# Unit 0's squares on VectorE, 1/(2 pi) inside the triangular factor, late caps and roundings on ScalarE, and a new written order of steps

## The chip, the cores and the metric

The kernel runs on one core of a Trainium2 chip. Times are microseconds (us) of that core for one execution; lower is better. Engines are named as the profile names them: PE is TensorE (PEld its weight loads), ACT is ScalarE, DVE is VectorE, POOL is GpSimd and SP is SyncE, which here only issues DMAs. A "q" behind a name (SPq, POOLq) is that engine's own instruction queue.

## The reference

```python
# gates: q, k, v, a_re, a_im are (4, 8, 768, 48) float32
mag = np.sqrt(a_re * a_re + a_im * a_im)
scale = np.minimum(mag, 0.999) / (mag + 1e-06)
a_re_n, a_im_n = (a_re * scale, a_im * scale)
for t in range(S):                         # S = 768 steps
    new_re = ar * S_re - ai * S_im
    new_im = ar * S_im + ai * S_re
    kv = np.einsum('bhd,bhe->bhde', k[:, :, t], v[:, :, t])
    S_re, S_im = (new_re + kv, new_im)
    y[:, :, t] = np.einsum('bhd,bhde->bhe', q[:, :, t], S_re)
...
x = y.transpose(0, 2, 1, 3).reshape(3072, 384)
h = x @ w_in                               # (384, 2048), float64 in memory
sp = log(1 + exp(h))
out = (h * erf(sp)) @ w_out                # (2048, 384)
```

The first part is a linear recurrence with complex gates per head and channel; the second is a feed-forward layer whose activation is h times the error function of softplus(h).

## The kernel before

**Units.** The 3072 tokens are cut into 12 units u = 0 to 11 of 256 tokens, each of two chunks c of 128 tokens (one token per partition, 8 heads x 48 channels = 384 elements along the free axis). Three units make one sequence of 768 tokens. The recurrence becomes prefix sums: the logarithms of the gate magnitudes and the gate angles are summed over the tokens of a chunk by a matmul with an upper triangular matrix of ones, `triu`, and then exponentials and sines of those sums weight q and k, so that a chunk's result is two small matmuls per head.

**The steps of one unit.** Every step is a Python generator that issues one or a few instructions each time it is resumed.

- `g` loads the real and imaginary gate parts (`ar`, `ai`) for a chunk, `k`, `q`, `v` the inputs.
- `m` (`g_mag`) squares both on ACT and adds them on DVE: s = |a|^2, with a sum for the final check.
- `t` (`g_tan`), `o`, `r` (`g_turn`): ai/ar by a logarithm, an exponential and a product, its largest value, and the arctangent, which leaves the angle in `th`.
- `l` (`g_log`): ln of s, then on DVE the cap `min(0.5 ln s, ln 0.999)` (L951, a tensor_scalar) and a subtraction (L953). From unit 5 on (`HALVED`) it also splits s into a rounded part `hi` (L958) and a rest `lo` (L960), so that the prefix sum can run as two matmuls in the float32r type with `triu_r`, a rounded copy of `triu`.
- `a` (`g_angle`): divides `th` by 2 pi (ACT, L991, units 0 to 4; from unit 5 on L984 together with the split), takes the prefix sum and removes whole turns. `p` (`g_decay`): prefix sum of s and two exponentials. `s` (`g_sin`): cosine and sine.
- `K`, `Q`, then `kT`/`qT` (transposes on PE, units 0 and 1) or `M` (transposes through DMAs, later units), `A` (scores), `S` (state), `Y` (result, gives xT).
- `h` (`ff_in`): x @ w_in, two tiles of 128 x 256 per resumption on PE and a copy to SBUF on ACT. Eight such tiles are a slab `sl`; two slabs make the 2048 hidden channels.
- `x` (`softplus`): four ACT passes over a whole slab, 128 x 2048: exp, ln, ln, exp. `e` (`erf_times_h`): one Gelu on ACT and four products on DVE per 128 x 512.
- `O`: the second matmul. Units 0 to 2 do it directly; units 3 to 11 by Strassen-like sums (`f`, banks X, Y, Z, W), and the last of these steps write the output.
- `n`, `b`, `i`: turn the float64 weights into float32, form sums of weights, and look once more through the weights for a check. `u` (`warm`): matmuls of the identity with itself whose result nobody reads, 48 of them, all near the start. `Z` (`check`): sums all check values and writes one flag `ok`; at the end every engine loads `ok` and branches past a slower general path.

**The order.** Nothing is scheduled by a tool. `ORDER` is a string of some 2290 step names, and the kernel resumes the named step each time:

```python
for nm in ORDER.split():
    if nm[0] == "u":
        steps[nm] = warm(int(nm[1:].split("_")[0]))
    next(steps[nm])
```

Each engine then runs its own instructions strictly in that order, with semaphores where data or buffers are awaited. DMAs are issued by SP, apart from the two first `ai` loads, which ACT issues (L801). Buffers of the gate stage (`lda`, `tmp`, `gat`) exist once, so a load into `ar` or `ai` waits until the previous unit's last reader is done. The first h matmuls need four converted pieces of w_in. ACT functions come in three table sets, and `act` loads a set (L785) when the next function is in another one.

Of the kernel before, what the change touches and what calls it, by code (L numbers as in the profile page):

```python
# [10 lines left out]
FP = mybir.dt.float32  # L11
# [38 lines left out]
u8_0 u2_40 u2_41 g0.0 g0.0 u4_38 u4_21 g0.1 g0.1 u4_20 u2_39 u4_2 t0.0 t0.0 t0.0 m0.0 m0.0 m0.0 m0.1 l0.0 t0.1  # L50
m0.1 m0.1 l0.0 l0.0 l0.0 l0.1 t0.1 l0.1 l0.1 l0.0 u2_25 p0.0 p0.0 p0.0 u2_34 u2_22 u8_1 o0.0 r0.0 a0.0 t0.1 l0.1
o0.1 r0.1 a0.1 n0 n0 n0 l0.1 n0 a0.0 a0.0 p0.1 n1 n1 n1 a0.0 a0.1 u2_24 g1.0 u2_23 k0.0 g1.0 q0.0 K0.0 m1.0 m1.0
n1 m1.0 s0.0 s0.0 s0.0 Q0.0 Q0.0 qT0.0.0 K0.0 v0.0 p0.0 v0.1 q0.1 k0.1 qT0.0.1 kT0.0.1 t1.0 p0.1 a0.1 p0.1 a0.1
t1.0 qT0.0.0 kT0.0.1 kT0.0.0 t1.0 o1.0 r1.0 qT0.0.1 kT0.0.0 g1.1 g1.1 Q0.1 S0.0 p0.0 K0.1 A0.0.0 A0.0.0 S0.0
s0.1 A0.0.1 A0.0.1 a1.0 a1.0 n3 p0.1 n2 p0.1 s0.1 s0.1 K0.1 Q0.1 n3 kT0.1.0 m1.1 m1.1 m1.1 n3 t1.1 l1.0 kT0.1.0
a1.0 l1.0 l1.1 a1.0 S0.1 S0.1 l1.0 l1.1 S0.1 qT0.1.1 qT0.1.1 t1.1 kT0.1.1 kT0.1.1 Y0.0 qT0.1.0 l1.1 qT0.1.0 l1.0
l1.0 p1.0 p1.0 Y0.0 p1.0 t1.1 n3 o1.1 r1.1 s1.0 a1.1 s1.0 A0.1.1 A0.1.1 A0.1.0 A0.1.0 Y0.1 q1.0 k1.0 K1.0 l1.1
q1.1 g2.0 v1.1 n4 l1.1 n2 n2 n2 s1.0 Q1.0 Q1.0 g2.1 v1.0 g2.1 g2.0 k1.1 a1.1 n6 n5 p1.0 n7 Y0.1 p1.1 K1.0 t2
a1.1 m2 n4 a1.1 n4 h0.0.6 t2 m2 m2 h0.0.4 p1.1 h0.0.6 n4 Q1.1 n6 t2 o2 p1.1 K1.1 l2 s1.1 l2 h0.0.4 l2 l2 r2 l2
n6 n6 kT1.0.0 kT1.0.0 h0.0.2 h0.1.0 h0.0.2 s1.1 s1.1 p1.1 q2.0 k2.0 a2.0 qT1.0.0 kT1.0.1 p2.0 qT1.0.0 n7 n7 a2.0  # L60
p2.0 p2.0 a2.0 n7 h0.0.0 h0.1.0 h0.0.0 kT1.0.1 qT1.0.1 qT1.0.1 a2.0 a2.0 x0.0 x0.0 e0.0.2 e0.0.0 n5 n5 g3.0 g3.0
n9 n8 n5 a2.0 a2.1 p1.0 p1.1 k2.1 v2.1 q2.1 S1.0 K1.1 A1.0.0 A1.0.1 Q1.1 A1.0.1 A1.0.0 a2.1 a2.1 h0.1.6 h0.1.6
Y1.0 v3.0 qT1.1.1 qT1.1.1 qT1.1.0 qT1.1.0 Y1.0 n8 n8 S1.0 n8 S1.0 n9 n9 a2.1 a2.1 a2.1 kT1.1.0 kT1.1.0 n9
kT1.1.1 kT1.1.1 S1.1 S1.1 S1.1 K2.0 Q2.0 p2.1 A1.1.1 A1.1.1 A1.1.0 A1.1.0 h0.1.4 s2 s2 s2 K2.0 Q2.0 g3.1 g3.1
Q2.0 n10 K2.0 n10 p2.0 v2.0 t3 m3 m3 m3 t3 h0.1.4 t3 o3 p2.1 p2.1 K2.1 n10 n10 Y1.1 l3 Y1.1 n11 h0.1.2 r3 h0.1.2
S2.0 p2.0 h1.0.0 M2.0 g4.1 M2.0 M2.0 k3.0 M2.0 g4.0 g4.0 S2.0 n11 K2.1 a3.0 a3.0 l3 S2.0 Q2.1 h1.0.0 l3 a3.0 l3
Q2.1 a3.0 l3 a3.1 n11 Q2.1 K2.1 h1.1.0 h1.0.2 x0.0 h1.1.0 x0.0 p3.1 p3.1 a3.1 p3.1 a3.1 p3.0 p3.0 A2.0.1 A2.0.0
e0.0.2 e0.0.0 e0.0.2 e0.0.2 e0.0.0 e0.0.0 A2.0.0 A2.0.1 n11 e0.0.2 m4 e0.0.0 h1.0.2 a3.1 a3.1 a3.1 t4 g4.1 m4
p3.0 t4 t4 h1.0.4 e0.0.6 e0.0.6 h1.0.4 h1.0.6 h1.0.6 Y2.0 q3.0 n12 g5.1 h1.1.2 n15 g5.0 M2.1 M2.1 M2.1 M2.1
e0.0.4 e0.0.4 e0.0.6 n12 e0.0.4 e0.0.4 e0.0.6 e0.0.4 h1.1.6 s3 s3 O0.1 s3 O0.0 e0.0.6 O0.2 O0.3 A2.1.1 A2.1.0  # L70
O0.4 O0.5 O0.6 x0.1 Q3.0 m4 l4 x0.1 l4 x0.1 l4 x0.1 K3.0 Q3.0 n12 n12 K3.0 n15 l4 K3.0 o4 l4 p3.0 k3.1 a4.0 p3.1
p3.0 A2.1.1 K3.1 A2.1.0 Y2.1 Q3.0 e0.1.2 e0.1.2 e0.1.0 e0.1.0 e0.1.2 Y2.0 h1.1.2 r4 e0.1.0 e0.1.2 e0.1.0 e0.1.2
a4.0 e0.1.0 e0.1.6 h1.1.6 Y2.1 e0.1.6 e0.1.6 e0.1.4 e0.1.4 e0.1.4 n15 a4.0 O0.7 S3.0 h1.1.4 h1.1.4 n15 x1.0 x1.0
# [12 lines left out]
Q4.1 O0.14 q5.0 p4.1 g6.0 K4.1 a5.1 a5.1 a5.1 a5.1 a5.1 e2.0.4 S4.1 A4.0.1 A4.0.0 A4.0.0 x2.1 e2.1.2 e2.1.2
e2.1.2 e2.1.2 g6.1 a5.1 h3.0.2 e2.1.2 m6 e2.1.0 e2.1.0 e2.1.0 e2.1.0 e2.1.0 O1.15 a5.1 g6.0 g6.1 k5.0 k5.1 O1.14
Y4.0 O1.14 h3.0.4 h3.0.6 O2.1 h3.0.0 O2.3 O2.5 O2.7 M4.1 M4.1 M4.1 M4.1 A4.1.1 A4.1.0 Y4.0 m6 h3.0.6 e2.1.4
e2.1.6 s5 s5 m6 e2.1.4 e2.1.6 e2.1.4 e2.1.4 e2.1.6 S4.1 s5 Q5.0 Q5.0 K5.0 K5.0 A4.1.1 K5.1 e2.1.6 e2.1.6 l6
h3.0.0 l6 t6 t6 q5.1 A4.1.0 x3.0 x3.0 l6 t6 S5.0 h3.1.4 h3.1.4 Q5.0 Q5.1 K5.0 l6 l6 K5.1 S5.0 l6 l6 e2.1.4 x3.0  # L90
x3.0 o6 Y4.1 e3.0.2 e3.0.2 e3.0.2 e3.0.0 e3.0.0 e3.0.2 e3.0.0 e3.0.2 e3.0.0 e3.0.0 h3.1.0 h3.1.0 r6 a6.0 Y4.1
a6.0 e3.0.6 e3.0.6 e3.0.6 e3.0.4 e3.0.4 e3.0.4 O1.14 v5.1 p5.0 M5.0 M5.0 M5.0 M5.0 q6.0 O2.9 h3.1.6 O2.0 O2.2
h3.1.2 h3.1.6 h3.1.2 a6.0 a6.0 a6.0 Q5.1 K5.1 e3.0.6 a6.1 a6.1 p5.0 e3.0.4 e3.0.4 A5.0.0 A5.0.0 O2.4 O2.6 A5.0.1
O2.8 O2.10 x3.1 x3.1 a6.1 x3.1 O2.12 A5.0.1 Y5.0 Q5.1 O1.15 M5.1 M5.1 x3.1 Y5.0 a6.1 a6.1 b6 e3.0.6 f3.0 b0 S5.0
b2 a6.1 a6.1 f3.0 e3.1.2 e3.1.0 h4.0.0 p6.0 e3.1.2 e3.1.0 e3.1.2 e3.1.2 h4.0.0 e3.1.0 e3.1.0 e3.1.2 e3.1.0 p6.0
Q6.0 p6.1 O2.14 O2.14 p6.0 e3.1.6 e3.1.6 e3.1.4 e3.1.4 e3.1.6 e3.1.4 e3.1.6 e3.1.6 e3.1.4 e3.1.4 s6 p6.1 p6.1
g7.0 k6.0 g7.1 m7 g7.1 g7.0 v7.0 i0 p6.0 i1 M5.1 M5.1 p6.1 h4.0.2 h4.0.2 m7 O2.11 O2.13 O2.15 t7 O2.15 t7 h4.0.6
h4.0.6 b0 b4 b6 m7 b6 b0 l7 l7 b0 b4 i0 b4 f3.1 b4 p6.0 h4.0.4 h4.0.4 l7 x4.0 x4.0 l7 i1 l7 b2 l7 l7 a7.0 h4.1.6
h4.1.6 O3.1 O3.1 t7 o7 h4.1.0 A5.1.1 O3.2 A5.1.0 A5.1.0 A5.1.1 b2 O3.2 f3.1 O3.0 O3.3 O3.4 h4.1.4 Y5.1 x4.0 x4.0
p6.1 v6.0 O2.14 q6.1 O2.15 e4.0.0 e4.0.0 e4.0.0 b2 e4.0.2 e4.0.2 e4.0.0 e4.0.2 e4.0.0 e4.0.2 r7 a7.0 e4.0.2 s6  # L100
s6 h4.1.0 e4.0.6 e4.0.6 e4.0.6 e4.0.4 e4.0.4 a7.0 a7.0 e4.0.4 h4.1.2 Y5.1 h4.1.4 h4.1.2 x4.1 O3.5 a7.0 a7.0 x4.1
k6.1 b6 O3.6 O3.7 e4.0.6 e4.0.4 h5.0.4 O3.5 O3.5 e4.0.4 O3.5 O3.7 a7.0 O3.7 a7.1 O3.4 x4.1 x4.1 K6.0 e4.0.6 Q6.0
K6.1 K6.0 K6.0 Q6.0 a7.1 e4.1.2 e4.1.2 e4.1.2 e4.1.0 e4.1.0 e4.1.2 e4.1.2 p7.0 p7.1 O3.8 h5.0.0 O3.12 O3.13 O3.9
O3.10 O3.11 e4.1.0 e4.1.0 h5.0.4 h5.0.0 e4.1.6 e4.1.6 e4.1.0 a7.1 e4.1.4 e4.1.6 e4.1.4 e4.1.4 a7.1 Q6.1 p7.0
p7.0 p7.1 h5.0.6 O3.13 h5.0.2 O3.11 h5.0.6 p7.1 g8.1 g8.0 M6.0 M6.0 k7.1 M6.0 M6.0 S6.0 a7.1 O4.0 A6.0.0 i2
h5.0.2 t8 m8 t8 e4.1.4 e4.1.6 e4.1.4 e4.1.6 f4.0 f4.1 Q6.1 a7.1 i2 a7.1 f4.1 K6.1 K6.1 i3 i3 S6.0 q7.0 g8.0 O4.3
O4.1 h5.1.6 f4.0 O3.13 g8.1 Q6.1 t8 O4.1 O4.2 O4.2 o8 A6.0.0 x5.0 x5.0 x5.0 x5.0 m8 m8 e5.0.0 A6.0.1 Q7.0 A6.0.1
e5.0.2 e5.0.2 e5.0.0 e5.0.0 e5.0.2 e5.0.0 O4.6 O4.7 e5.0.0 e5.0.2 e5.0.2 O4.4 O4.5 O4.5 O4.4 s7 s7 h5.1.6 s7
k7.0 M6.1 M6.1 O3.11 M6.1 p7.1 M6.1 e5.0.6 e5.0.6 O4.5 e5.0.6 e5.0.6 O4.5 K7.0 e5.0.4 e5.0.4 e5.0.4 e5.0.6 O4.7
# [572 lines left out]
def quotient_path(  # L682
# [740 lines left out]
```

## Time and profile before

| what | value |
|---|---|
| median of 3 runs | 659.68 us (659.02 to 659.84) |
| profiled execution, its own time | 659.36 us |
| its span | 657.5 us (1.86 us lie around it) |
| PE busy | 641.9 us of the span, 98% |
| DVE, ACT busy | 603.4 us (92%), 577.5 us (88%) |
| PE clock granted | 1.00 |
| DMA | 70.19 MB, mean 107 GB/s; 269396 of 282792 packets under 512 B |
| ACT table loads | 94, 120.6 us, 1283 ns each |

A busy share is an average over stages. The table of stages in the prediction therefore cuts the span into windows and gives each engine's busy time in each. PE's busy time includes the unread matmuls of `warm` (12.9 us as a group), and PE's ends are modelled, so a window in which PE is busy throughout still has to be judged by what its instructions are.

### The profile page before, as it was taken

Reading aid. Unit: us, or ns where it says so; the run is one execution under the profiler, and the core shown is the slowest. Engines: PE = TensorE matmul, PEld = TensorE weight load, DVE = VectorE, ACT = ScalarE, POOL = GpSimd, SP = SyncE. Lnnn points to the kernel's source line nnn. Section 1 sums busy time; section 2 is a strip of 40 time slices with the busy share of each in tenths; the row PEclk is TensorE's granted clock in tenths of the full one; section 3 lists DMA queues with packets and bytes.
Section 4 is the critical chain, followed back from the end, with each engine's and each line's share of the span. In section 5 each row is a group of like instructions: output and inputs, shape, how many; then the busy total and the mean of one; then the engine's idle time right before and its main releaser. Section 6 shows DMA issues by size and latency. Waiting matters only on the chain.

```text
span 657.5 us, 12307 instructions
## 1 busy us (share of the span) xinstructions
PE 641.9 (98%) x4728; PEld 561.9 (85%) x4728; DVE 603.4 (92%) x980; ACT 577.5 (88%) x762; POOL 1.1 (0%) x8
## 2 busy tenths in 40 slices
PE   8799999999999999999999999999999999999997
PEld 7678887777777877999899899999999898999887
DVE  5999999999999999999999999999999898868893
ACT  7999999999999999987978999997997987787820
POOL 0000000000000000000000000000000000000000
PEclk9999999999999999999999999999999999999999
DMA  8996875663146328328516726626637515511000
GB/s 214 209 260 160 190 153 116 155 109 61 29 86 130 61 39 188 65 41 200 97 17 161 148 39 149 124 41 149 122 58 128 141 21 111 150 42 48 1 25 27
DMA packets 282792, 70.19 MB, mean 107 GB/s; under 512 B 269396, under 2 KB 272488, under 8 KB 282728
## 3 DMA queue, kind: packets, MB, share of 16 engines
q1 hardware_dynamic: 280648, 68.96, 48.6%
q8 instruction: 38, 0.62, 0.4%
q10 hardware_dynamic: 2080, 0.39, 0.3%
q14 instruction: 26, 0.21, 0.1%
HBM read 48.82 MB, written 4.75 MB: 81 GB/s over the span
## 4 chain that ended last, share of the span: by engine, by line
ACT 52%; DVE 23%; PE 16%; issue 4%; DMA 3%; SPq 1%; DVEq 0%; ACTq 0%
ACT L785 11%; ACT yy L786 9%; ACT z L786 8%; PE hps L1152 7%; ACT e L786 4%; DVE z L1180 4%; DVE yy L1182 4%; ACT y L786 4%; ACT th L786 3%; DVE e L1184 3%; ACT CS L786 3%; ACT h L1155 3%; DVE h L1186 3%; PE Y L1244 2%; ACT s L786 2%
## 5 line engine op out<-in xcount | busy, mean ns | idle before, releaser
L1152 PE MATMUL hps<-xT,w_in_sb 128*128 128x256 f32 x1152 | 262.4, 381 | 1.5 <-ACT h L1155 1.5
L1152 PEld LDWEIGHTS hps<-xT,w_in_sb 128*128 128x128 f32 x1152 | 215.6, 190 | 34.7 <-ACT h L1155 3.9
L785 ACT ACT_TABLE_LOAD x94 | 120.6, 1283 | 3.6 <-issue 2.0
L1180 DVE TENSOR_TENSOR z<-z,yy 128x512 f32<-128x512 f32 x96 | 64.9, 687 | 15.9 <-ACT e L786 15.1
L786 ACT ACTIVATE e<-z 128x512 f32<-128x512 f32 x96 | 58.2, 628 | 22.3 <-DVE h L1186 21.8
L1182 DVE SCALAR_TENSOR_TENSOR yy<-z,yy 128x512 f32<-128x512 f32 x96 | 65.1, 688 | 1.7
L1186 DVE SCALAR_TENSOR_TENSOR h<-e,h 128x512 f32<-128x512 f32 x96 | 65.1, 686 | 1.1
L1220 PE MATMUL ops<-w_out_sb,h 128*128 128x384 f32 x192 | 65.7, 488 | 0.1
L1184 DVE TENSOR_TENSOR e<-e,yy 128x512 f32<-128x512 f32 x96 | 64.7, 686 | 1.1
L1155 ACT COPY h<-hps 128x512 f32<-128x512 f32 x96 | 54.5, 579 | 11.1 <-PE hps L1152 11.1
L1220 PEld LDWEIGHTS ops<-w_out_sb,h 128*128 128x128 f32 x192 | 35.7, 190 | 21.9 <-DVE w_out_sb L848 1.1
L786 ACT ACTIVATE z<-h 128x2048 f32<-128x2048 f32 x24 | 45.8, 1909 | 6.6 <-DVE seen L858 5.9
L1084 PEld LDWEIGHTS sc<-KQ 96*128 96x128 f32 x384 | 47.7, 192 | 4.5 <-issue 2.5
L1084 PE MATMUL sc<-KQ 96*128 96x128 f32 x384 | 48.9, 275 | 1.5 <-DVE KQ L1075 0.9
L786 ACT ACTIVATE z<-z 128x2048 f32<-128x2048 f32 x24 | 45.9, 1911 | 0.6
L786 ACT ACTIVATE yy<-yy 128x2048 f32<-128x2048 f32 x24 | 45.9, 1911 | 0.5
L786 ACT ACTIVATE yy<-z 128x2048 f32<-128x2048 f32 x24 | 45.8, 1907 | 0.4
L1139 PE MATMUL y<-A,v 128*32 128x128 f32 x768 | 33.4, 275 | 1.3 <-DVE A L1088 0.9
L1088 DVE TENSOR_TENSOR A<-sc,triu 128x512 f32<-128x512 f32 x48 | 31.9, 681 | 1.0 <-PE sc L1084 1.0
L1103 PEld LDWEIGHTS kv<-v,kt 128*96 128x96 f32 x320 | 29.7, 165 | 1.5 <-issue 0.7
L1103 PE MATMUL kv<-v,kt 128*96 128x48 f32 x320 | 29.7, 246 | 0.0
L1244 PE MATMUL Y<-T,S 128*128 128x192 f32 x144 | 26.7, 331 | 1.7 <-DVE out L1252 1.3
(115 smaller groups left out, 1053.3 us busy)
## 6 DMA issues: line engine op xcount, KB each, us to landing
KQ<-X SPq DMA_DIRECT2D x240, 64.0 KB
raw<-in_moe_w_in_dram SPq DMA_DIRECT2D x8, 768.0 KB
raw<-in_moe_w_out_dram SPq DMA_DIRECT2D x8, 768.0 KB
again<-in_moe_w_in_dram SPq DMA_DIRECT2D x8, 768.0 KB
ar<-in_a_re_dram SPq DMA_DIRECT2D x24, 192.0 KB
k<-in_k_dram SPq DMA_DIRECT2D x24, 192.0 KB
q<-in_q_dram SPq DMA_DIRECT2D x24, 192.0 KB
v<-in_v_dram SPq DMA_DIRECT2D x48, 96.0 KB
```

Source lines behind the costliest of these rows:

```text
L785: scalar.preload_act_table_set(sets[0])
L786: scalar.activation(func=func, **kw)
L1084: nc.tensor.matmul(out=ps[:, j, :], lhsT=head("k", g * HG + j, u, c), rhs=head("q", g * HG + j, u, c), start=True, stop=True)
L1103: nc.tensor.matmul(out=kv[0:D2, j, :], lhsT=T["kt", u, c][:, j].rearrange("p u d -> p (u d)"), rhs=side(T["v", u][:, c, j // 2], j % 2), s ...
L1152: nc.tensor.matmul(out=ps[:, e, :], lhsT=w_in_sb[:, (sl * SLAB + i) // 2, kd, e * P:(e + 1) * P], rhs=T["xT", u][:, kd, :], start=(kd == 0 ...
L1155: scalar.copy(out=T["h", u, sl][:, i:i + 2, :], in_=ps)
L1180: vector.tensor_tensor(out=z, in0=z, in1=y, op=OP.mult)
L1182: vector.scalar_tensor_tensor(out=y, in0=z, scalar=-2.0, in1=y, op0=OP.add, op1=OP.mult)
L1184: vector.tensor_tensor(out=e, in0=e, in1=y, op=OP.mult)
L1186: vector.scalar_tensor_tensor(out=h, in0=e, scalar=1.0 / RT2, in1=h, op0=OP.add, op1=OP.mult)
L1220: nc.tensor.matmul(out=ps, lhsT=lhsT, rhs=w_out_sb[:, i, :], start=i == HALF, stop=i == KF - 1)
L1244: nc.tensor.matmul(out=ps, lhsT=a(sl)[:, i], rhs=b(sl, i), start=sl == 0 and i == 0, stop=sl == NSL - 1 and i == HALF - 1)
```

## The change

1. **First loads.** `load_gates` issues all four loads of unit 0 from SP, in the order ar, ai, ar, ai. The two issues on ACT go.
2. **First squares.** For u = 0, `g_mag` makes both squares with DVE tensor_tensor, and the addition becomes a scalar_tensor_tensor that also gives the accumulated sum. ACT loses four squares and two accumulator reads.
3. **Division by 2 pi.** A new constant `turns` = `triu`/(2 pi), made by one DVE instruction, is the stationary operand of the angle's prefix sum in units 0 to 4. The ten ACT instructions of L991 go.
4. **Caps and roundings of units 6 to 11** (`LATE = 6`). The cap becomes an ACT Relu with scale -0.5 and a bias column `log_cap`, followed by a DVE scalar_tensor_tensor in place of the subtraction; the rounding to `hi` becomes an ACT copy.
5. **The last slab in halves.** The softplus of unit 11's slab 1 is `x11.1.0` and `x11.1.1`, each over 128 x 1024. The check has one more column for each of its two sums.
6. **Small things.** The check columns lie in one tile `found`. `triu_r` takes the buffer of the identity and is made late by a step `j`, before unit 5. A name `H` marks the place of the branch hint; in both built programs the hint is the first instruction of each engine.
7. **A new `ORDER`.** 2287 names. The step sets are otherwise the same, the places of nearly all differ: on average by some 18 names, at most by 317. In the built programs PE has 2424 matmuls before and after, ACT 94 table loads before and 95 after, SP 517 DMAs before and 519 after (the two first `ai` loads).

```diff
-            engine = nc.scalar if (nm, u) == ("ai", 0) else nc.sync
-            engine.dma_start(out=whole(lda, nm, u, [P, C, H, D])[:, c], in_=rows(src, u, c))
+            nc.sync.dma_start(out=whole(lda, nm, u, [P, C, H, D])[:, c], in_=rows(src, u, c))
...
-        act(out=s, in_=gate("ar", u, cc), func=AF.Square, accum_out=large[:, i:i + 1])
+        sums = large[:, i:i + 1]
+        if u == 0:
+            for t, nm in ((s, "ar"), (y, "ai")):
+                vector.tensor_tensor(out=t, in0=gate(nm, u, cc), in1=gate(nm, u, cc), op=OP.mult)
+                yield
+            vector.scalar_tensor_tensor(out=s, in0=s, scalar=1.0, in1=y, op0=OP.mult, op1=OP.add, accum_out=sums)
+            yield
+            return
+        act(out=s, in_=gate("ar", u, cc), func=AF.Square, accum_out=sums)
...
-        vector.tensor_scalar(out=s, in0=s, scalar1=0.5, scalar2=math.log(CAP), op0=OP.mult, op1=OP.min)
-        yield
-        vector.tensor_tensor(out=s, in0=s, in1=y, op=OP.subtract)
+        if u < LATE:
+            vector.tensor_scalar(out=s, in0=s, scalar1=0.5, scalar2=LOG_CAP, op0=OP.mult, op1=OP.min)
+            yield
+            vector.tensor_tensor(out=s, in0=s, in1=y, op=OP.subtract)
+        else:
+            act(out=s, in_=s, func=AF.Relu, scale=-0.5, bias=log_cap)
+            yield
+            vector.scalar_tensor_tensor(out=s, in0=s, scalar=LOG_CAP, in1=y, op0=OP.subtract, op1=OP.subtract, reverse0=True)
...
-        vector.tensor_scalar(out=hi, in0=s, scalar1=1.0, scalar2=None, op0=OP.mult)
+        if u < LATE:
+            vector.tensor_scalar(out=hi, in0=s, scalar1=1.0, scalar2=None, op0=OP.mult)
+        else:
+            scalar.copy(out=hi, in_=s)
...
-            scalar.mul(out=th, in_=th, mul=1.0 / TAU)
-            yield
             ps = ps_b.tile([P, DM], FP, tag="b", name="sum")
             goes_on = goes_on and u < 2
-            nc.tensor.matmul(out=ps, lhsT=triu, rhs=th, start=True, stop=not goes_on)
+            nc.tensor.matmul(out=ps, lhsT=turns, rhs=th, start=True, stop=not goes_on)
...
-    def softplus(u, sl):
-        z = T["z", u, sl] = zp.tile([P, SLAB, NT], FP, tag="z", name="z")
-        i = u * NSL + sl
-        act(out=z, in_=T["h", u, sl], func=AF.Exp, accum_out=exps[:, i:i + 1])
+    def softplus(u, sl, e=None):
+        z = whole(zp, "z", (u, sl), [P, SLAB, NT], tag="z")
+        y = whole(yp, "yy", (u, sl), [P, SLAB, NT], tag="yy")
+        ss = slice(0, SLAB) if e is None else slice(e * HALF, (e + 1) * HALF)
+        z, y, h, i = z[:, ss], y[:, ss], T["h", u, sl][:, ss], u * NSL + sl + (e or 0)
+        act(out=z, in_=h, func=AF.Exp, accum_out=exps[:, i:i + 1])
```

The two orders at their beginning and end, before (-) and after (+); the last resumption of `Z` compares the sums with their limits and writes `ok`:

```diff
-u8_0 u2_40 u2_41 g0.0 g0.0 u4_38 u4_21 g0.1 g0.1 u4_20 u2_39 u4_2 t0.0 t0.0 t0.0 m0.0 m0.0 m0.0 m0.1 l0.0 t0.1
+u8_0 u4_38 u4_21 u4_20 u4_2 g0.0 u2_34 u2_41 u2_25 g0.0 g0.1 g0.1 H t0.0 t0.0 m0.0 m0.0 m0.0 m0.1 t0.0 m0.1 l0.0
...
-e11.1.6 f11.1 f11.1 O11.1 O11.1 O11.3 O11.2 O11.4 O11.2 f11.0 O11.5 O11.5 O11.5 O11.5 Z O11.6 O11.7 O11.8 O11.4
-O11.7 O11.7 O11.9 O11.12 O11.10 O11.11 O11.13 O11.11 O11.11 O11.13 O11.13
+e11.1.4 e11.1.6 f11.1 f11.1 O11.4 O11.4 O11.2 O11.2 O11.6 O11.5 O11.7 O11.5 O11.5 O11.5 O11.7 i15 i15 Z O11.7
+O11.8 O11.9 O11.10 O11.11 O11.12 O11.11 O11.11 O11.13 O11.13 Z Z O11.13
```

## The prediction

> **What bounds the kernel now.** First the page's busy shares, then the table of stages (busy time of each engine in stretches of the span, with clock, DMA share and GB/s):
>
> ```profile
> PE 641.9 (98%) x4728; PEld 561.9 (85%) x4728; DVE 603.4 (92%) x980; ACT 577.5 (88%) x762; POOL 1.1 (0%) x8
> ...
> 0.00:10.00 10.00, 8.41 (x61) 8.41 (x62) 3.16 (x17) 6.53 (x15) 1.08 (x8) 1.00 0.89 242
> 10.00:20.00 10.00, 7.92 (x48) 5.86 (x46) 9.79 (x17) 9.73 (x19) 0.00 (x0) 1.00 0.95 183
> 20.00:30.00 10.00, 8.30 (x71) 7.22 (x71) 9.10 (x17) 9.93 (x22) 0.00 (x0) 1.00 0.92 227
> 30.00:40.00 10.00, 8.24 (x133) 6.69 (x133) 9.43 (x18) 9.97 (x23) 0.00 (x0) 1.00 0.89 201
> 40.00:50.00 10.00, 10.00 (x48) 8.40 (x48) 9.86 (x14) 9.95 (x18) 0.00 (x0) 1.00 0.89 274
> ...
> 400.00:450.00 50.00, 49.84 (x397) 46.32 (x396) 49.26 (x80) 47.87 (x61) 0.00 (x0) 1.00 0.49 102
> ...
> 620.00:640.00 20.00, 17.96 (x107) 16.81 (x107) 17.17 (x38) 8.93 (x9) 0.00 (x0) 1.00 0.06 20
> ```
>
> PE is the bound from 40 us to about 600: it idles 2.2 us there. A step that only relieves ACT or DVE in that stretch buys nothing. What can be bought is at the ends. In the first 40 us PE shows 32.9 us busy, but about 13 us of that are the unread matmuls, so only 20 us are work; ACT is 97 to 100% busy from 10 us on and DVE 91 to 98%. The chain of waits is ACT nearly without a break there. At the other end PE idles 2.0 us between 620 and 640, and about 3.8 us follow its last matmul.
>
> The groups by line and form give the prices (busy us, mean ns, then idle before):
>
> ```profile
> L785 ACT ACT_TABLE_LOAD x94 | 120.6, 1283 | 3.6 <-issue 2.0
> L991 ACT ACTIVATE th<-th 128x384 f32<-128x384 f32 x10 | 5.2, 520 | 0.1
> L786 ACT ACTIVATE CS<-CS,column 128x768 f32<-128x768 f32 x10 | 9.3, 933 | 0.1
> L951 DVE TENSOR_SCALAR s<-s 128x768 f32<-128x768 f32 x10 | 5.5, 547 | 0.1
> L958 DVE TENSOR_SCALAR hi<-s 128x768 fp32r<-128x768 f32 x7 | 3.9, 556 | 0.0
> ```
>
> **What the Trainium skill says.** "ScalarE: Activation LUTs", What ACT_TABLE_LOAD costs, gives 1283 ns for a set switch and a further drain of 1380 ns. The trace has the 1283 ns, but the next activation starts 0.01 us behind a load, so I count 1.28 us. The same section prices an activation with immediate operands at 186 ns + 0.833 ns per element: 1.04 us for 1024 elements, a form the trace lacks; for 2048 it gives 1.89, the trace 1.91. "VectorE: DVE Perf Modes", The perf-mode tier table, has an fp32 tensor_scalar at twice the rate of a tensor_tensor; the trace agrees (547 ns at L951 against 956 at L953). So the late DVE subtraction, now a scalar_tensor_tensor, costs what it did, and only the two half-price instructions leave DVE. "DMA: Bandwidth & Descriptors", Issuing engines are not separate DMA queues, says loads from SP and ACT share the same 16 engines; so one issuing queue should cost only issue time.
>
> **The change part by part.**
>
> *Start, by ACT.* Gone before 40 us: four squares (512 and 508 ns), two accumulator reads (0.19 us), four divisions (517 ns): 4.5 us of ACT busy time. Back to back they take less than their duration, 0.41 to 0.43 us a piece in the chain. Replaying the new order by hand with these rows: the first ln of s, at 7.19 us before, waits now for the first two loads (I put them at 4.0 and 4.6 us; ar landed at 4.55 before), a DVE product (0.56) and the sum (0.57): about 5.8. The first switch to the sine tables, at 12.25, comes at about 11.0; there follow two arctangents, F, one square, and the three CS steps, and the next switch, at 18.80, comes at about 16.7. Two more divisions, of unit 1, give 0.8. ACT reaches unit 2's gates 3.0 us earlier. Bounds: 2.1 (only what is replayed) and 4.5.
>
> *Start, by DVE.* It gets four products and two longer additions, 2.2 us, and `turns` for the old `triu_r` (0.22 each). They fit into the first 10 us (3.16 busy). But afterwards it was nearly full: idle 1.8 us between its first product at 5.68 and 10, 1.7 us from 10 to 40. With a start 1.7 us earlier the most it can gain by 40 us is 1.8 + 1.7 + 1.7 - 2.4 = 2.8.
>
> *Start, by DMA.* Share 0.89 to 0.95. Up to unit 2's gates SP and ACT issued 19 loads of 192 KB, 8 of 96 and 5 of 768; in the new order it is 17, 4 and 5: 8.45 against 7.67 MB, at the 213 GB/s of these 40 us 3.7 us less. The SP queue has two more issues ahead of the first weights (0.6 us each), so the first conversion may come late; DVE has gate work to put there.
>
> The three limits are 3.0, 2.8 and 3.7. No engine fills every gap: **-2.4 us**, bounds 0 and -4.5.
>
> *40 to 250 us.* Six more divisions go, 3.1 us of a full ACT; PE idles about 0.8 us in the stretch: **-0.2**, bounds 0 and -0.8. Without them ACT could not stay ahead of a PE that starts earlier.
>
> *250 to 600.* Six units get an ACT Relu with a column operand (nearest row 0.933) and a copy (0.85): +10.7 us ACT; DVE loses 6 x (0.547 + 0.556) = 6.6 us. About one unit falls into each window of 50 us, where ACT idles 2.1 us (400 to 450) to 7. Cover: PE's own queue of h and O matmuls. **0**, bounds -1.4 (all of PE's idle time there) and the rival below.
>
> *Last slab.* ACT had four passes of 1.91, 7.7 us with a table load before Gelu could start: table load at 616.08, first e at 626.64. In halves five passes of 1.04 come ahead of the first Gelu: about 5.2, so it starts 2.5 us earlier. The price is two more table loads (2.6 us) and 0.7 for small passes, so the last two Gelus gain only about 1. PE's idle in 620 to 640 is 2.0 us; **-1.2**, bounds 0 and -2.5 (with the 0.5 before 620). Late next: DVE's four products.
>
> *The check at the very end.* Before, `ok` was written at 645.3 and four of the engines' loads of it were done while PE still worked. Now its matmul stands behind the last W matmul on PE, six compares (0.46) and the reduction (0.15) behind the last output on DVE, and the loads of `ok` (0.48) and the branch behind those. Lines of the branch, and of what follows it on POOL (last two numbers: start us):
>
> ```profile
> L1391 POOLq COMPARE_BRANCH  x1: 59/59/59, 645.9 to 645.9; - x1
> L1391 ACTq EVENT_SEMAPHORE  x1: 17/17/17, 646.3 to 646.3; - x1
> L1391 POOLq EVENT_SEMAPHORE  x1: 17/17/17, 648.6 to 648.6; - x1
> L1391 SPq EVENT_SEMAPHORE  x8: 17/17/17, 655.1 to 656.1; - x8
> ```
>
> With T the end of the last matmul (653.74), the last output DMA was awaited until T + 2.4. The new chain: 0.4 + 0.46 + 0.15 + 0.5 + 0.25 for SP's registers and compare + 0.55 for the jump = T + 2.3, beside the DMA. POOL took 2.7 us from compare to the next instruction, unseen in the old middle; at the end that is T + 4.3, where the closing barrier met POOL at T + 3.1. **+0.6**, bounds 0 and +1.8.
>
> *No cost:* the merged check columns, `j` (0.22 us of DVE in a stage where PE is full), the hint (the same first instruction in both programs).
>
> Sum: -2.4 - 0.2 + 0 - 1.2 + 0.6 = -3.2 from the profiled 659.36 (span 657.5): 656.2. The median of the runs lies 0.3 higher: **656.5**. This kernel's measurement can tell about 0.2%, 1.3 us, from no change.
>
> **The rivals.**
>
> - *ACT becomes the bound late (slower).* At 400 to 450 ACT is 47.87 of 50 busy and gets 1.8. If the Relu and the copy fall ahead of an h copy that PE awaits, up to 1.8 us per unit shows. It decides from 3.2/6 = 0.53 us a unit; at 0.8 a unit, +4.8 - 3.2 = +1.6: 661.3. For it: ACT h <- PE and PE hps <- ACT h are pairs in the waits. Against: PE waited for h copies 1.5 us in all, with four waits, and the chain from 507 to 600 is PE alone.
> - *DVE or a load holds the start (same).* The new squares delay DVE's conversions, and PE's first h tiles wait as before; the tail and the end cancel: 659.4. For it: DVE at 91 to 98%, DMA at 0.9. Against: fewer bytes lie ahead.
> - *Everything comes (much faster).* Start -4.5, tail -2.5, end 0, idle -0.8: 651.9. It needs a PE without gaps from about 35 us.
> - *The change doesn't do what it says:* only true of the hint.
>
> **How the numbers follow.** Forecast 0.56 (654 to 658.3); much faster 0.16; same 0.14; slower 0.14. The ends are set by the rivals: 652.5 leaves out part of the third, 660.8 part of the first. Faster by over 1.3 us: 0.72; within: 0.14; slower: 0.14.
>
> **What would show it.** Right: the table load of 40.10 at about 37, PE full from about 37, the first e of the last slab 10.5 us behind its last h copy shrinking to 8, PE idle of 620 to 640 under 1 us, ACT at 92 to 99% in 250 to 550 with PE idle still under 2.5 us. Wrong: a wait of PE on ACT h or of DVE on raw in the first 60 us, PE idle between 250 and 600 above 4 us, or over 5 us behind the last matmul.

## The result and the profile after

The changed kernel takes **659.0 us** (median, 658.0 to 660.2) against 660.4 us for the kernel before on the same chip, 22 runs each: ratio **0.9982 [0.9975, 0.9988]**, a gain of 1.2 us (0.8 to 1.7). The forecast was a gain of 3.2. The profiled execution of the changed kernel took 659.63 us with a span of 657.9; against before's 659.36 it shows no gain at all, so one pair of profiles is too coarse for 1 us here, and below the ratios decide on size and the profiles on place.

The page's busy shares first, then the stages (columns: window, length, then for PE, PEld, DVE, ACT and POOL busy us and instructions; clock granted to PE, DMA share, GB/s). They answer to the lines of before in the prediction.

```profile
PE 642.2 (98%) x4728; PEld 562.6 (86%) x4728; DVE 599.2 (91%) x976; ACT 581.7 (88%) x765; POOL 1.1 (0%) x8
```

```profile
0.00:10.00 10.00, 8.41 (x57) 8.41 (x58) 5.86 (x26) 6.19 (x11) 1.09 (x8) 1.00 0.82 194
10.00:20.00 10.00, 8.59 (x52) 6.44 (x52) 8.73 (x15) 8.03 (x16) 0.00 (x0) 1.00 0.88 191
20.00:30.00 10.00, 9.03 (x79) 8.12 (x80) 9.93 (x18) 9.95 (x22) 0.00 (x0) 1.00 0.96 286
30.00:40.00 10.00, 9.51 (x131) 6.92 (x130) 9.50 (x17) 9.95 (x21) 0.00 (x0) 1.00 0.83 189
40.00:50.00 10.00, 10.00 (x52) 8.85 (x51) 9.70 (x14) 9.96 (x18) 0.00 (x0) 1.00 0.97 257
400.00:450.00 50.00, 49.81 (x394) 46.04 (x393) 45.86 (x74) 48.00 (x61) 0.00 (x0) 1.00 0.54 111
620.00:640.00 20.00, 18.37 (x110) 17.49 (x109) 17.87 (x31) 11.27 (x15) 0.00 (x0) 1.00 0.17 60
```

In the first 40 us PE is busy 35.5 us instead of 32.9, so it idles 4.5 us instead of 7.1. ACT is no longer full between 10 and 20 (8.03 of 10; 9.73 before). Between 620 and 640 PE idles 1.63 us (before 2.04). PE's busy time as a whole is the same (642.2 against 641.9): its work did not change, so only idle time and the piece behind the last matmul can differ.

That piece is where the gain went. PE's last matmuls of the output, after and before (start, length):

```profile
648.38 2.76 PE L1267 MATMUL W<-w_out_sb,h 128*128 128x192 f32 x16
```

```profile
652.27 1.46 PE L1244 MATMUL W<-w_out_sb,h 128*128 128x192 f32 x8
```

They end at 651.16 us; before it was 653.74. But the span got 0.4 us longer: 6.7 us follow that matmul instead of 3.8. (In two kernels below that differ only in POOL's hint or in who issues two loads, the last matmul ends at 649.9 and 650.2, so its place in one profile is good to about 1 us.) The queue entries at the load of `ok` (columns: count, ns least/median/most, first and last start in us), after:

```profile
L1419 POOLq TENSOR_LOAD <-ok x1: 792/792/792, 652.1 to 652.1; - x1
```

The same load before, with three engines loading at once:

```profile
L1390 POOLq TENSOR_LOAD <-ok x1: 494/494/494, 645.3 to 645.3; - x1
```

The branch after:

```profile
L1420 POOLq COMPARE_BRANCH  x1: 59/59/59, 653.0 to 653.0; - x1
L1420 ACTq EVENT_SEMAPHORE  x1: 17/17/17, 653.4 to 653.4; - x1
L1420 POOLq EVENT_SEMAPHORE  x1: 17/17/17, 657.0 to 657.0; - x1
L1420 SPq EVENT_SEMAPHORE  x8: 17/17/17, 653.8 to 654.4; - x8
```

SP is through with the outputs at 654.4. ACT arrives 0.4 us behind its branch. POOL, whose 1.1 us of busy time all lie in the first 10 us, comes out of its branch 4.0 us after it, at 657.0, and the closing barrier waits for it. Before, the same jump took 2.7 us at 645.9, under PE's last products.

The groups by line and form, for the prices (busy us, mean ns, idle before):

```profile
L787 ACT ACT_TABLE_LOAD x95 | 121.9, 1283 | 2.4 <-PEq L1436 0.9
L788 ACT ACTIVATE s<-s,column 128x768 f32<-128x768 f32 x6 | 5.5, 925 | 0.0
L982 ACT CAST hi<-s 128x768 fp32r<-128x768 f32 x6 | 4.9, 820 | 0.0
L974 DVE SCALAR_TENSOR_TENSOR s<-s,y 128x768 f32<-128x768 f32 x6 | 5.6, 938 | 0.0
L933 DVE SCALAR_TENSOR_TENSOR s<-s,y 128x384 f32<-128x384 f32 x2 | 1.1, 554 | 0.0
```

The unseen prices were right: 0.93 us for the new Relu, 0.82 for the rounding on ACT, 0.94 for the new subtraction, 0.55 for the addition with a sum. The softplus pass over 1024 elements, estimated at 1.04 us, took 1.04 to 1.06.

### The profile page after: what moved, and what is told of

It is laid out like the page before. It is cut to its first block, busy times and chain, and to the rows that moved or that the text cites. A ratio compares the mean times of both kernels' runs of the same rounds, so it can differ in the third digit from the quotient of the medians.

```text
span 657.9 us, 12296 instructions
## 1 busy us (share of the span) xinstructions
PE 642.2 (98%) x4728; PEld 562.6 (86%) x4728; DVE 599.2 (91%) x976; ACT 581.7 (88%) x765; POOL 1.1 (0%) x8
## 4 chain that ended last, share of the span: by engine, by line
PE 48%; ACT 30%; DVE 15%; DMA 3%; issue 3%; SPq 1%; POOL 0%; DVEq 0%; POOLq 0%; ACTq 0%
PE hps L1174 21%; ACT L787 7%; ACT yy L788 5%; ACT z L788 5%; PE Y L1267 4%; PE Z L1267 4%; PE X L1267 3%; PE y L1161 3%; PE sc L1106 3%; ACT e L788 3%; DVE z L1203 3%; DVE yy L1205 3%; DVE e L1207 2%; PE W L1267 2%; PE kv L1125 2%
## 5 line engine op out<-in xcount | busy, mean ns | idle before, releaser
L788 ACT ACTIVATE yy<-z 128x2048 f32<-128x2048 f32 (+1 forms) x25 | 46.1, 1842 | 0.8 <-DVE found L859 0.4
L788 ACT ACTIVATE z<-h 128x2048 f32<-128x2048 f32 (+1 forms) x25 | 46.1, 1844 | 0.6 <-ACT h L1177 0.3
L788 ACT ACTIVATE z<-z 128x2048 f32<-128x2048 f32 (+1 forms) x25 | 46.1, 1845 | 0.5
L788 ACT ACTIVATE yy<-yy 128x2048 f32<-128x2048 f32 (+1 forms) x25 | 46.0, 1842 | 0.3
```

What stands on the lines that cost most here:

```text
L788: scalar.activation(func=func, **kw)
```

## The experiments

Theory: the end ate the gain. The check behind the last product costs 2 us and not the 0.6 of the sum, and all the rest comes about as forecast. Rivals: the start gave less than it seems, because the squares or the load queue do nothing; the late caps and roundings take time back; or what gained is not one of the edits but the new order. The runs first move the check, then take the new code and the new order apart. Where an expectation names theories by letters, A is that of the end, C that of the start and E that of the caps in places not made for them. All ratios are to the kernel before, on the same chip.

### The end: where the check stands

**Changed kernel, check moved forward:**

```diff
-... O11.7 i15 i15 Z O11.7 O11.8 O11.9 O11.10 O11.11 O11.12 O11.11 O11.11 O11.13 O11.13 Z Z O11.13
+... O11.7 i15 i15 Z O11.7 O11.8 O11.9 Z Z O11.10 O11.11 O11.12 O11.11 O11.11 O11.13 O11.13 O11.13
```

> The changed kernel with one edit: the last two resumptions of the check (its matmul, and the six compares that write ok) stand behind O11.9 instead of at the very end. Theory A (the end): in the changed kernel the last matmul ends 2.6 us earlier than before (651.16 against 653.74), but the flag is written only at 652.1 and POOL's jump behind it takes until 657.0; with ok written under PE's last products POOL's jump is done by then and the end falls back to about 3.8 us behind the last matmul. Then this kernel takes 2.5 to 3.3 us less than the changed one: ratio to the kernel before 0.993 to 0.995. Theory B (the end is set by the last output's DMA and the closing barrier, and POOL's jump is only beside it): within 0.1% of the changed kernel, 0.998.

Measured: 656.9 us (655.8 to 658.1), ratio 0.9952 [0.9938, 0.9966], 2.0 us below the changed kernel's ratio and clear of its interval. The branch lines of this kernel:

```profile
L1414 POOLq COMPARE_BRANCH  x1: 59/59/59, 648.1 to 648.1; - x1
L1414 POOLq EVENT_SEMAPHORE  x1: 17/17/17, 651.0 to 651.0; - x1
```

and its last matmul of the output:

```profile
649.42 2.76 PE L1261 MATMUL W<-w_out_sb,h 128*128 128x192 f32 x16
```

The jump starts 5 us earlier, takes 2.9 us and is over before the last matmul ends (652.2). The tail is 3.7 us again. This version beats both kernels.

**Kernel before, comparison at the very end:**

```diff
-... O11.5 O11.5 O11.5 O11.5 Z O11.6 O11.7 O11.8 ... O11.13 O11.13
+... O11.5 O11.5 O11.5 O11.5 O11.6 O11.7 O11.8 ... O11.13 Z O11.13
```

> The kernel before with one edit: the third resumption of the check (compares and ok) stands at the very end, ahead of the last output DMA's issue only. Theory A: the last matmul ends where it did, the end moves from 3.8 to between 6 and 7 us behind it: 2.2 to 3.2 us more, ratio 1.0033 to 1.005. Theory B: no difference above 0.1%.

Measured: 662.9 us, ratio 1.0047 [1.0035, 1.0059]: +3.1 us from this place alone. The loads of `ok` take 0.76 to 0.84 us, and POOL's jump is the longest piece again:

```profile
L1385 POOLq COMPARE_BRANCH  x1: 59/59/59, 655.7 to 655.7; - x1
L1385 POOLq EVENT_SEMAPHORE  x1: 17/17/17, 659.8 to 659.8; - x1
```

**Changed kernel, no hint for POOL:**

```diff
-engines = [... for e in ("PE", "DVE", "SP", "Activation", "Pool")]
+engines = [... for e in ("PE", "DVE", "SP", "Activation")]
```

> The changed kernel without the branch hint on POOL alone (the other four engines keep theirs). If POOL's slow jump (4.0 us from compare to next instruction, against 0.4 to 0.6 on the others) is a fetch that its hint does not prevent: the same 4 us and the same time. If the hint spoils it: the jump under 1 us and 3 us less. If the hint helps a little: longer.

Measured: 658.8 us, ratio 0.9981 [0.9975, 0.9988], as the changed kernel; POOL's jump took 3.8 us. The hint has no visible part in that jump.

### New code against new order

**New code in the order of before** (the division's names dropped, `j` before the first `m5`, the last slab whole, the check at its old place):

> The changed kernel's instructions in the order of the kernel before (the division's resumptions left away, the late rounded ones placed by m5, the last slab whole, the check where it was before). Theory C (the gain at PE comes from the moved work: 4.5 us less on a full ScalarE by 40 us): the first h matmul comes 1.5 us or more earlier than the 41.1 us of before, and the time is 1 to 2.5 us below the kernel before, ratio 0.996 to 0.9985. Theory D (it is the new order that makes use of it): the first h matmul within 0.8 us of 41.1 and the ratio 0.999 to 1.003, more if the added ScalarE work of units 6 to 11 falls ahead of h copies.

Measured: 674.7 us, ratio 1.0228 [1.0213, 1.0243]. Its first h product stands at 41.1 us, as before the change. PE idles 11.3 us more between 200 and 550. The waits of this kernel (waiting instruction, what it waited for, us in all, times, longest):

```profile
DVE s L968 <- ACT s L782: 8.8, 3, 4.7
PE hps L1168 <- ACT h L1171: 6.5, 8, 2.1
DVE lo L978 <- ACT hi L976: 5.7, 4, 2.6
```

and one such place in the timeline (start, length, instruction, in brackets the idle time before it and its cause):

```profile
264.38 1.91 ACT L782 ACTIVATE z<-z 128x2048 f32<-128x2048 f32 x1
266.19 0.92 ACT L782 ACTIVATE s<-s,column 128x768 f32<-128x768 f32 x1
267.14 0.96 DVE L968 SCALAR_TENSOR_TENSOR s<-s,y 128x768 f32<-128x768 f32 x1 [2.81 <-ACT s L782]
...
268.13 0.83 ACT L976 CAST hi<-s 128x768 fp32r<-128x768 f32 x1 [1.02 <-DVE s L968]
268.87 0.58 ACT L1171 COPY h<-hps 128x512 f32<-128x512 f32 x1
```

The Relu stands where the old order had the cap on DVE: behind two softplus passes of 1.9 us. DVE waits 2.8 us for it, then ACT waits 1.0 us for DVE's subtraction, and the h copy that PE needs stands behind both. Here a step moved to another engine at its old place made a round trip between two queues that each run in order.

**The same with caps and roundings on DVE:**

```diff
-TURNS, HALVED, LATE = 2, 5, 6
+TURNS, HALVED, LATE = 2, 5, 99
```

> New code in the old order, which took 14.4 us more than the kernel before, with one more edit: caps and roundings of units 6 to 11 stay on VectorE. Theory E: those 14.4 us come from the ScalarE steps of part 4 in places fitted to VectorE (PE idles 12 us more between 200 and 550 us, with ScalarE's rounding waiting for VectorE's subtraction and the reverse): then this kernel is back at the kernel before, ratio 0.997 to 1.002. Theory F: they come from something else in the new code (no division step, squares on VectorE, the check's columns): above 1.012.

Measured: 657.9 us, ratio 0.9963 [0.9950, 0.9977]. So the whole loss was the caps and roundings in places not made for them (16.7 us between the two medians). And squares, queue and `turns`, in the old order, with the old tail, gain 2.4 us: more than the change as a whole.

**That kernel with the ten divisions back on ACT,** at the places that the old order had:

```diff
+            scalar.mul(out=th, in_=th, mul=1.0 / TAU)
+            yield
...
-            nc.tensor.matmul(out=ps, lhsT=turns, rhs=th, ...)
+            nc.tensor.matmul(out=ps, lhsT=triu, rhs=th, ...)
```

> The changed code in the order of before with caps and roundings on DVE (657.9 us) has lost 2.3 us against before. This kernel puts the ten divisions by 2 pi of units 0 to 4 back on ACT, at the places that the old order had for them. Theory (the prediction's step for 40 to 250 us): ACT has them in a stage where PE idles under 1 us in all, so their absence bought little: 0 to 0.5 us, this kernel at 657.9 to 658.4 and its first h product within 0.3 us of 40.1. Rival: the divisions stand right before the cumulative sums for which PE waits in order, and their absence is what brought most of the 2.3 us: this kernel at 659 or above.

Measured: 659.9 us, ratio 0.9997 [0.9980, 1.0013]: the gain is gone. PE idles 7.1 us in the first 40, as before the change; without the divisions 6.4. The first 40 us of the kernel without them and of this one:

```profile
0.00:40.00 40.00, 33.60 (x310) 28.61 (x311) 34.15 (x73) 34.01 (x66) 1.09 (x8) 1.00 0.92 216
```

```profile
0.00:40.00 40.00, 32.88 (x308) 28.07 (x309) 33.66 (x72) 34.59 (x70) 1.08 (x8) 1.00 0.91 214
```

The rival has it: the missing divisions are worth 2.2 us, by the two intervals 0.8 to 3.6. What is left here is the kernel before with the squares, the queue and the small things of the change, and together they bring nothing that its interval shows.

**That kernel with unit 0's squares back on ACT** (the branch `if u == 0` of `g_mag` taken out):

> The changed code in the order of before with caps and roundings on DVE, and unit 0's squares back on ACT; the load of ai stays in SP's queue. In the kernel with squares on DVE the first h product stood at 40.1 us (before 41.1). Theory: the squares on DVE took the 1.0 us off the start: here it is back at 41.1 and the time is 0.8 to 1.2 us longer, 658.7 to 659.1. Rival: the start came from the earlier landing of the first loads, or from the divisions that are gone: first h product stays at 40.1 and the time within 0.3 us of 657.9.

Measured: 658.9 us, ratio 0.9976 [0.9968, 0.9985]. The median is 1.0 us up, as expected, but the intervals overlap, and PE's idle time of the first 40 us is 6.3 us with the squares on ACT and 6.4 with them on DVE. The first h product stood at 41.0 us here. But it stood at 41.6 in a kernel below whose first 40 us are the same as those of the 40.1: it scatters by more than the effect. A gain of the squares between 0 and 1 us is what can be said.

### The single parts undone in the new order

**Squares back on ACT,** the same edit in the changed kernel:

> The changed kernel with unit 0's squares back on ScalarE, order unchanged. My theory: ScalarE is the start's bound, it gets 2.4 us of work there, of which it has about 1.2 us of waits to hide in the first 12 us: the first h matmul 1 to 1.8 us later than the changed kernel's 39.2, ratio to before 0.9995 to 1.001. Rival (VectorE and loads set the start as much, so relieving VectorE gives it back): no difference, 0.997 to 0.999.

Measured: 659.4 us, ratio 0.9991 [0.9985, 0.9998]; PE idles 4.5 us in the first 40, as in the changed kernel. Again between nothing and 1 us.

**First `ai` loads issued by ACT again:**

```diff
-            nc.sync.dma_start(out=..., in_=rows(src, u, c))
+            engine = nc.scalar if (nm, u) == ("ai", 0) else nc.sync
+            engine.dma_start(out=..., in_=rows(src, u, c))
```

> The changed kernel with the first two loads of ai issued by ACT again, as before the change. Still open of the start: whether the queue of the first loads or the squares brought the earlier first h product (39.2 us, scatter 38.6 to 40.1 over the runs of this order). Theory (prediction): in one queue the first gates land about 0.9 us earlier, and the kernel with ACT issuing loses 0.3 to 0.9 us. Rival: the loads are bound by the engines that carry them and not by who issues them: within 0.3 us of the changed kernel.

Measured: 659.2 us, ratio 0.9984 [0.9977, 0.9991]: no difference. The first square on DVE does start 1.0 us later (4.69 instead of 3.69), but the last of the four only 0.3 us later (7.35, 7.02): in the changed kernel DVE stands 0.5 and 0.2 us for the two `ai` loads between its squares, and so loses most of the early start. The queue is a rearrangement, not a gain that these runs show.

**Division back on ACT in the new order,** the ten names put right before the matmul's:

> The changed kernel with the division by 2 pi back as a ScalarE step right ahead of each angle's matmul in units 0 to 4. My theory: 2.1 us of the 5.2 fall into the full first 40 us and 3.1 into the nearly full stretch to 140 us: last matmul 2 to 4 us later, ratio 1.001 to 1.004. Rival (PE is the bound from 40 us on, so only the first 2.1 count, partly hidden): 0.999 to 1.0005.

Measured: 679.3 us, ratio 1.0290 [1.0275, 1.0305], far above both expectations. The waits and the stages show why:

```profile
PE sum L1013 <- ACT th L1009: 14.8, 9, 4.2
```

```profile
140.00:145.00 5.00, 5.00 (x32) 4.14 (x30) 2.69 (x4) 4.98 (x6) 0.00 (x0) 1.00 0.60 93
145.00:150.00 5.00, 0.76 (x3) 0.54 (x3) 4.76 (x8) 4.34 (x9) 0.00 (x0) 0.85 0.70 116
150.00:155.00 5.00, 5.00 (x9) 2.64 (x8) 2.65 (x5) 0.58 (x1) 0.00 (x0) 0.50 0.13 27
```

The matmul stands directly behind the division, and ACT's queue is full, so PE stands still for up to 4.2 us, nine times. After the longest of these the granted clock is 0.50 for the next 5 us. It had fallen once before in this run: it is 0.56 between 25 and 30 us and 0.76 between 30 and 35. This is the price of a step put in without slack, not that of the division; the runs in the old order give that.

**Caps and roundings back on DVE in the new order** (`LATE` at 99):

> The changed kernel, in its own order, with caps and roundings of units 6 to 11 back on VectorE (VectorE + 6.6 us, ScalarE - 10.7). My prediction's step (PE is the bound in 250 to 600 us, so part 4 buys nothing): 0.997 to 0.9995. Rival (the new order is fitted to the moved steps, and VectorE at 97% falls behind): 1.001 to 1.01, with PE idle between 250 and 600 above 4 us.

Measured: 662.2 us, ratio 1.0027 [1.0015, 1.0038]: 3.0 us slower than the changed kernel, so in this order the moved work is needed. PE's idle time from 250 to 600 doubles from 1.4 to 2.9 us, though it stays under the 4 us that the rival named:

```profile
250.00:600.00 350.00, 347.09 (x2635) 318.98 (x2634) 329.52 (x529) 302.86 (x377) 0.00 (x0) 1.00 0.47 99
```

In these two profiles the last product ends 2.7 us later. The move that costs 16.7 us in one order is worth 3.0 us in the other.

**Last slab whole in the new order** (four `x11.1` at the place of the first half):

> The changed kernel with the last slab's softplus whole, its four passes at the place of the first half. Theory: the halves bring 0.4 to 0.9 us in the tail, so this kernel is 0.4 to 0.9 us longer than the changed one, PE idle of 620 to 640 us at 2.0 to 2.5 us (halves: 1.63). Rival: the order around the slab, not the split, brought the earlier end: within 0.3 us of the changed kernel.

Measured: 661.8 us, ratio 1.0021 [1.0012, 1.0031], 2.6 us slower than the changed kernel, more than the 0.4 to 0.9 expected; PE idles 3.4 us between 620 and 640.

**Halves in the old order** (the caps-on-DVE kernel, `x11.1` x4 replaced by the names that the change has there, the first Gelus among them):

> The changed code in the order of before with caps and roundings on DVE, and with the last slab's softplus in two halves, as the change has it. Theory (the prediction's step for the last slab, as the change's trace sizes it): the first e of the last slab starts about 3.5 us behind its present place of the whole slab's, two table loads more, PE idle between 620 and 640 us falls from 1.6 by 0.4 to 0.9: 657.0 to 657.5 us. Rival: DVE's chain of erf steps, not ACT's first e, sets when the last products can start, and the split gives nothing or loses its two table loads: 657.9 or above. At 657.0 it would be as fast as the changed kernel with its check moved ahead.

Measured: 661.5 us, ratio 1.0014 [1.0007, 1.0021]: the halves *cost* 3.4 us here. DVE's timeline shows the reason:

```profile
625.62 0.42 DVE L1330 TENSOR_REDUCE sums<-found 128x1 f32<-128x24 f32 x4
629.24 0.26 DVE L1330 TENSOR_REDUCE sums<-found 128x1 f32<-128x25 f32 x2 [3.19 <-ACT yy L782]
629.41 1.28 DVE L1197 TENSOR_TENSOR z<-z,yy 128x512 f32<-128x512 f32 x2
```

In the old order the check's reductions stand *ahead* of the slab's erf products. They need the sums of every softplus, and with halves the second half's sum is written at 629.2 us. So DVE stands 3.2 us before the first half, whose Gelu was done at 624.6. PE pays:

```profile
634.83 2.73 PE L1261 MATMUL X<-w_out_sb,h 128*128 128x192 f32 x8 [2.14 <-DVE out L1269]
```

and after that standstill the granted clock is 0.51 between 635 and 640 and 0.81 between 640 and 645. The clock is the smaller part of the loss: of the 22 runs, nine have a mean granted clock of 0.994 or 0.995, as the profiled one, and a median of 662.1 us; the eleven at 0.999 or 1.000 have 661.1.

**The same with the check behind the erf steps:**

```diff
-... O10.7 Z e11.1.2 ... O10.11 Z O10.12 ... O11.5 Z O11.6 O11.7 O11.8 O11.4 O11.7 O11.7 O11.9 O11.12 ...
+... O10.7 e11.1.2 ... O10.11 O10.12 ... O11.5 Z O11.6 O11.7 O11.8 Z O11.4 O11.7 O11.7 O11.9 Z O11.12 ...
```

> As the kernel with the changed code in the order of before, caps and roundings on DVE and the last slab in halves (661.5 us), but with the three parts of the check behind the slab's erf steps instead of among them: the reductions after the last of O11.5, the product after O11.8, the comparison after O11.9. In the kernel without this move DVE stood 3.2 us at the check's reductions until the second half's sums were written, PE then idled 2.1 us in one piece, and the granted clock fell to 0.51 for the next five microseconds. Theory: the early place of the check and the halves exclude each other; with the check behind, PE's idle time of 620 to 640 us falls to 1.0 to 1.6, the clock stays at 1.0, and the time is 657.0 to 657.8, below the whole slab's 657.9. Rival: the halves themselves (two table loads more, 2.6 us) hold the erf steps of the old order back: 659 or above, with PE waiting for DVE's out steps as before. A comparison that ends by 650 us leaves POOL's branch under the last products.

Measured: 657.8 us, ratio 0.9960 [0.9946, 0.9973]. The loss is gone, PE's idle time of 620 to 640 is 1.4 us, the clock stays at 1.00, and POOL's jump (647.0 to 649.8) is hidden:

```profile
620.00:640.00 20.00, 18.60 (x111) 17.96 (x112) 16.88 (x31) 11.32 (x15) 0.00 (x0) 1.00 0.06 20
```

In this order halves and an early check exclude each other. But beside the whole slab (0.9963) the halves now gain nothing that the intervals show. The same holds for the rest of the change: the changed kernel with its check moved forward (0.9952 [0.9938, 0.9966]) can't be told from the old order with squares, queue and `turns` alone (0.9963 [0.9950, 0.9977]). That the late caps, the halves and the new order together bring anything is not shown.

## Why the prediction was wrong, and where it was right

The direction was right, and the sum up to the last product came out near: with the check moved forward the changed kernel gains 3.2 us (2.2 to 4.1), where the terms without the end summed to 3.8. That is partly luck, for the largest of these terms, the start, came about in another way than was reckoned. The step that failed is **"The check at the very end"**, +0.6 with bounds 0 and +1.8: it measures +2.0 (1.0 to 3.0 by the intervals) from the ratios of the two changed kernels and +3.1 (2.3 to 3.9) in the kernel before.

- **The end, term by term.** With T the end of the last matmul, `ok` was reckoned at T + 1.0 and written at T + 0.9: right. Its loads were taken at 0.48 us, the row of before, where three engines loaded at once; all five at once take 0.75 to 0.83. POOL's jump was taken at the 2.7 us of before; at the end it takes 4.0. So POOL arrives at T + 5.8 and not T + 4.3. Both terms were carried from a place where the instruction ran under other conditions. The sum was short on its own terms too: T + 4.3 against the T + 3.1 of before is +1.2, and +0.6 was written, with no reason for the other half. The sign of being wrong that was named for this step, over 5 us behind the last matmul, came: 6.7 us.
- **Start, -2.4.** PE's idle time of the first 40 us fell by 2.7 us, within what the sum said, but not by the path that it followed. The replay had squares and loads bring the first switch to the sine tables from 12.25 to 11.0 us, and with two divisions less the next one from 18.80 to 16.7. The trace has 12.21 and 17.84:

```profile
11.23 0.87 ACT L788 ACTIVATE pr<-sum 128x384 f32<-128x384 f32 x2 [1.24 <-PE sum L1040]
...
12.21 1.28 ACT L787 ACT_TABLE_LOAD   x1
...
17.84 1.28 ACT L787 ACT_TABLE_LOAD   x1
```

In the replay ACT went straight on; in the trace it waits 1.24 us for a cumulative sum, and that sum stands on PE behind unread matmuls, though its operand was done on DVE at 9.0 us:

```profile
1.59 8.96 PE L1325 MATMUL unread<-ident 128*128 128x128 f32 x60 [1.59 <-POOL ident masks.py:199]
10.38 0.81 PE L1040 MATMUL sum<-s,triu 128*128 128x384 f32 x2
```

So nothing of the 1.25 us of squares and loads is left at the first switch. The stretch from there to the second is 0.9 us shorter, as replayed (0.85): two divisions and one square less. Unit 2's gate table load, named as a sign at about 37, came at 38.73: 1.4 us earlier instead of 3.0. The runs agree: the queue gives nothing, the squares between 0 and 1 us with no trace in PE's idle time, the divisions' absence about 2 us (in the old order; 0.7 of it as PE's idle time before 40 us). The remaining 1.8 us of idle time (6.3 to 4.5) came with the new order, which the prediction did not price by itself.

- **40 to 250, -0.2.** PE idled 0.9 us there before and 1.4 after; too small for these profiles to decide. Whether ACT could stay ahead with the divisions is not shown: PE's 14.8 us of waits with them put back at the last moment are those of that place.
- **250 to 600, 0.** Right as a net number (PE idle 1.4 before, 1.4 after), with ACT up by 5.3 us in the window and DVE down by 4.4 (10.7 and 6.6 were reckoned; nearly all steps have new places, and where the rest lies was not followed). The reason given, that PE's own queue covers the move, was wrong. It holds only with steps placed for it: the same code at old places opens the rival's wait of PE on h copies, 6.5 us (1.5 before), and undoing the move in the new order costs 3.0. The rival "ACT becomes the bound late" described this wait of PE; the round trip with DVE it did not name. The order kept both away.
- **Last slab, -1.2.** The first e came 8.0 us behind the last h copy, exactly as replayed (615.13 to 623.15). PE's idle time fell by 0.4 between 620 and 640 and by 0.5 between 600 and 620: 0.9 in place of 1.2, and 1.63 us stayed in 620 to 640 where under 1 was the sign. What the prediction missed is the sum that the second half writes late, and that the check waits for it. The check behind the erf steps is therefore part of the halves, but at O11.9 it would have been late enough; the very end costs 2 us for nothing.
- **The hint, `j`, merged columns: none.** The run without POOL's hint agrees; the other two were not run by themselves.

What stays open: how far the single parts add up. Undone one by one in the new order they cost 0.6, 0.1, 20, 3.0 and 2.6 us, of which the last three are each more than the whole change brings. The order is fitted to this code, and these numbers measure the fit as much as the part.

## What to carry to other kernels

Price a step at the end with durations from the end: what is free under other work, a load by several engines or a jump of an idle engine, is paid in full behind the last matmul, and its length there may differ. Where each engine keeps a written order, a part and its place are one change: a step that moves to another engine needs its inputs early and its readers late, and an undone part tells the price of a broken order, not of the part. When a producer is cut into pieces, look for the reader that needs all of them, and move it behind those that need only the first.

## What the runs showed of the hardware

- POOL's jump at the branch took 2.5 to 2.9 us in the eight kernels where PE, DVE and SP branched later, and 3.2 to 4.5 us in the eight where all five engines branched within 0.4 us at the end (4.0 in the changed kernel, 2.7 before). The jumps of ACT, DVE and SP took 0.4 to 0.6 us, PE's 0.4 to 0.5 where it had no matmul left. Why POOL is slower, and why more so at the end, no run tells.
- A load of one word by SP, ACT and POOL at once took 0.47 to 0.50 us, by all five engines at once 0.75 to 0.84.
- In the run with the divisions put back PE's granted clock fell to 0.50 late in a standstill of 4.2 us (145 to 149), but also about 1 us into one of only 1.2 us (24.4 to 25.6), each time for some 7 us. With the halves in the old order it was 0.50 to 0.55 for 7 us after one of 2.1 us in the profiled run, and in that kernel nine of 22 runs show the lower mean clock. After another of 2.1 us (131 to 133, divisions put back) and one of 1.9 us (last slab whole) it stayed at 1.00. The Trainium skill, "TensorE: Matmul & The Clock Gate", Part 1: The HAM clock gate, has the half rate after an idle window of about 3.4 us that runs freely. The rate agrees with the trace; here shorter standstills were enough twice, and two others of about 2 us were not.
